# Softmax steps of the eighth b placed inside the last stage's h tiles, state rows stored from SyncE, output copies dealt out anew

## The chip, the cores and the metric

One core of a Trainium2 chip runs the whole program. The metric is the device time of one execution in microseconds, as the median of several executions; lower is better. The engines are named as in the profile: PE (TensorE), DVE (VectorE), ACT (ScalarE), POOL (GpSimd) and SP (SyncE, which issues nearly all transfers).

## What is computed

Three blocks follow one another. `x` is 8 x 8 x 512 x 64, `state` 8 x 8 x 32 x 64; after the first block there are 8 b's of 512 token rows and 32 state rows each, 512 wide.

```python
# attention between the tokens and the state, both ways
a  = softmax(x @ state.T / 8);   xread = a @ state
a2 = softmax(state @ x.T / 8);   sread = a2 @ x
# a wide layer with a clipped quadratic
h = x @ w_in                                   # 512 -> 2048
g = where(h >= 1, h, where(h <= -1, 0, (h + 1) ** 2 / 4))
x = g @ w_out                                  # 2048 -> 512
# soft mixture: 8 experts with 4 slots each
logits = x @ phi                               # 4608 x 32
d = softmax(logits, axis=0);  slot_input = d.T @ x
slot_out[e] = relu(slot_input[e] @ w1[e]) @ w2[e]
out = softmax(logits, axis=1) @ slot_out
```

All data are 32-bit floats. The softmax over axis 0 runs over all 4608 rows, so the experts can start only when the last row is in.

## The kernel before

The kernel works in stages b = 0 to 7, one for each b's 512 tokens, and a last stage b = 8 for the 256 state rows of all b's. In a stage, 16 h tiles (m = 0 to 15, `hstep`) of 128 hidden units each are multiplied on PE; ACT, DVE and POOL turn each into its part of g. In stage 8 an h tile is 12 matmuls of 128 x 256 (line 547, numbered k = 0 to 11): `w_in`'s columns are split in a high and a low part by `wsplit` one tile ahead, into two alternating buffers, on the engines that a table names. The h tiles have three PSUM banks in turn.

`estep(b, k)` multiplies four g tiles into the logits E (four groups to a b; the last group of b runs in stage b + 1). `smblock(b)` then does the running softmax over rows in steps, a generator that the stage's loop steps on:

1. eS is copied out of E (ACT).
2. LR, a group of eight matmuls that turn eS; then the maximum bm and nm (DVE), the exponential back into eS (ACT), and small copies.
3. dRp, four transposes of eS on PE, copied to dR (ACT).
4. `fall`: 64 matmuls of dR with `gp`, the buffer that holds this b's g, into the banks FV and FX; eight DVE instructions add them to `acc`.
5. for b = 7 alone, `merge`: Mp, P and Sp on PE fold the four partial accumulators; after it the places of `gp` and `acc` are given to loads of expert weights.

In stage 8 of the kernel before, the loop steps the block of b = 7 on once after each of the h tiles m = 1, 2, 3, 4, 5. Stages 2 to 7 have PE's order written out by hand. Stage 8 has not: there a planner orders every engine's instructions by priority (program order, with raised priority inside a group) and by the times of a model, so that a step can stand some matmuls behind its place in the text.

Expert weights (w1 and w2, 16 slices of 1 MB each) are loaded by SP into whatever place falls free (`give`, `prefetch`, line 820); most of the places come from this very stage: the `gp` units after `fall`, `acc` after P, the `win` buffers after the last splits that read them, the split buffers after the last h tile, the buffers of transposed g after the group P of `smstate`. SP works in order, so a load whose place is not free yet holds up the loads behind it.

At the end `combine` multiplies the slot outputs with the token weights into four PSUM banks at a time (two of one V tile and two others, or two X, one E, one H), copies the banks to `o` by DVE and ACT in turn (line 1138), and stores `o`: b's 0 to 5 in two column halves, b's 6 and 7 whole. The state rows (b = 8, two banks) are stored by eight POOL transfers of 64 KB each, between the stores of b = 6 and b = 7.

Of the kernel before, what the change touches and what calls it, by code (L numbers as in the profile page):

```python
# [13 lines left out]
PSUM = bass.MemoryType.PSUM  # L14


CFG = {'gg': 1, 'ns': 1, 'do': 0, 'no': 1, 'nl': 0, 'n0': (1, 12), 'nw': 512, 'nj': 'CABD', 'cw': (2, 2, 2, 4, 5, 6, 6, 7, 8, 8, 9, 11, 12, 13, 14, 15), 'pr': (0, 3, 4, 6), 'a0n': 4, 'w1p': (), 'r0': 3, 'sw': 1, 'whole': (6, 7), 'em': 8, 'lE': (0, 5, 8, 11), 'sV': (0, 4, 9, 12), 'sE': (7, 11, 15), 'sS': (1, 3, 5, 7), 'sN': 13, 'sM': (14, 14), 'gv7': 'EESEESSEEESSEEEE', 'cpos': (0, 0, 1, 1, 2, 2, 3, 7, 8, 9, 10, 10, 13, 14), 'at0': (4, 4, 7, 7, 9, 13, 14, 15, 15, 15), 'lP0': ((1, 1), (2, 1), (3, 1)), 'lP1': ((1, 0), (1, 1), (2, 0), (2, 1), (3, 0)), 'gv1': 'EEEEEEEEEESEEEES', 'f32': (0, 1, 2, 3), 'wsm': 14, 'xsP': 1, 'eng': ('PE',), 'wt8': (7, 8, 9, 10, 11, 12, 13, 14), 'wte': 'DA', 'wb': 12, 'gv6': (3, 5, 15), 'lP': ((0, 0), (0, 1), (1, 0), (2, 0), (3, 1)), 'attA': (3, 4, 7, 9, 9, 9, 11, 12), 'attB': (1, 11, 11, 12, 13), 'attN': (14, 15), 'dv': (3, 7, 8), 'fl': -0.484375, 'hp': 2000, 'att7': (3, 5, 6, 7, 8, 10), 'og': 1, 'n3': 1, 'n3m': 10, 'wS': ('AP', 'PP', 'AD', 'AP', 'DP', 'DP', 'PP', 'DD', 'AP', 'DP', 'AD', 'AP', 'DD', 'AD', 'DD', 'DP'), 'xsm': 12, 'k0': 0, 'rg': 6, 'spg': 0, 'att0': 6, 'att': 7, 'V0': (1, 3, 4), 'Vn': (0, 3, 9), 'Vx': 12, 'wn': 'H', 'wsev': 'adad', 'conv': (4, 8, 9, 11, 12, 13, 19, 21, 24, 26, 28, 32, 36, 40, 44, 48, 52, 56, 60), 'todo': [1, 1, 1, 2, 0, 0, 0, 3, 0, 0, 2, 2, 1, 1, 0, 0], 'E0': ((0, 8), (0, 14), (0, 14), (0, 15)), 'T0': ((0, 12), (0, 14), (0, 15), (1, 0)), 'sm0': 6, 'E': 1, 'sm': 1, 'tqB': (5, 9, 13), 'GP': 0, 'pe': (3,), 'psH': 3, 'gtpX': (0, 7), 'tq0': (13, 15), 'keep': (2, 3, 4, 5), 'x2': (1, 3), 'natm': 1, 'warm': 26, 'bounce7': (0, 3), 'split': 1, 'wt': 0, 'so': '111000000000ccc111111', 'smm': (0, 0, 1, 2, 8, 10, 12), 'tqv': (), 'tqvm': 0, 'first': 'x', 'apath': 2, 'f32c': 1, 'place': 1, 'attm': (3, 6, 7, 8, 9, 12), 'subPm': True, 'loDm': False, 'bounce': (0, 1, 2, 3), 'bq': ('s', 's'), 'xq': 's', 'nat': ((1, 11), (2, 2), (2, 3), (2, 11), (3, 2), (3, 4), (3, 9), (4, 2), (4, 3), (4, 9), (5, 2), (5, 3), (5, 9), (6, 2), (6, 4), (6, 9)), 'subP': (1,), 'mulD': (), 'loD': (), 'qlag': 0, 'gv0': 'ESSESEEESEEEEEEE', 'gv': 'EEEEEEESEEEESEEE', 'gvS': 'BEBBBEEESSSBEBBB'}


@with_exitstack  # L20
def kernel(
# [157 lines left out]
        stage_load(nxt(i))  # L179

    wps, wD = {}, {}

    def conv_wo(i):

        g, h = divmod(i - 8, 2)
        if h == 0:
            wD[g] = rot_g.tile([128, 4, 512], F32, tag="g", name="wD")
        words(i, wD[g][:, 2 * h:2 * h + 2, :].rearrange("p k f -> p (k f)"))
        stage_load(nxt(i))
        if h == 1:  # L190
            wps[g] = psX.tile([128, 512], F32, tag="X", name="wps")
            group([dict(out=wps[g][32 * k:32 * k + 32, :], lhsT=phi_t[:, k, :], rhs=wD[g][:, k], start=True, stop=True)
                   for k in range(4)], [made[0], made[1]])
            sb = rot_q.tile([128, 512], F32, tag="q", name="wsb")
            act(sb, wps[g])
            wpp = wps[g][:, 0:128].rearrange("p (x n) -> p x n", x=4)
            for x in range(4):
                mm(out=wpp[:, x, :], lhsT=sb[:, 128 * x:128 * x + 128], rhs=R4, start=True, stop=True)
            act(wp[:, 4 * g:4 * g + 4, :], wpp)

    def nat_load(u, at):
        if u < 8:
# [321 lines left out]
    def hstep(b, m):  # L524
# [105 lines left out]
    def smblock(b):  # L630
# [89 lines left out]
    def fall(b, al, dR):  # L720
# [226 lines left out]
    for b in range(B + 1):  # L947
# [14 lines left out]
        for m in range(NM):  # L962
# [156 lines left out]
    def combine(dh, groups):  # L1119
# [4 lines left out]
        for n, bs in groups:  # L1124
# [80 lines left out]
```

## Time and profile before

| | |
|---|---|
| median of 3 executions | 477.71 us (477.7 to 478.51) |
| the profiled execution | 476.62 us |
| its span in the trace | 474.8 us |
| PE busy | 92% of the span |
| DVE, ACT, POOL busy | 79%, 61%, 52% |
| transfers issued by SP (q1) | 93.00 MB |
| transfers issued by POOL (q0) | 0.52 MB |

The trace is that of the profiled execution; its times are counted from the start of the span. A busy share is an average over stages with different limits, so it is read stage by stage. Stage 8's h tiles start at about 363 us; the stores end at about 472 us.

### The profile page before, as it was taken

Reading aid. Unit: us, or ns where it says so; the run is one execution under the profiler, and the core shown is the slowest. Engines: PE = TensorE matmul, PEld = TensorE weight load, DVE = VectorE, ACT = ScalarE, POOL = GpSimd, SP = SyncE. Lnnn points to the kernel's source line nnn. Section 1 sums busy time; section 2 is a strip of 40 time slices with the busy share of each in tenths; the row PEclk is TensorE's granted clock in tenths of the full one; section 3 lists DMA queues with packets and bytes.
Section 4 is the critical chain, followed back from the end, with each engine's and each line's share of the span. In section 5 each row is a group of like instructions: output and inputs, shape, how many; then the busy total and the mean of one; then the engine's idle time right before and its main releaser. Section 6 shows DMA issues by size and latency. Waiting matters only on the chain.

```text
span 474.8 us, 10761 instructions
## 1 busy us (share of the span) xinstructions
PE 436.8 (92%) x4352; PEld 249.5 (53%) x4352; DVE 372.8 (79%) x664; ACT 288.6 (61%) x526; POOL 245.4 (52%) x222
## 2 busy tenths in 40 slices
PE   4699999999999999999999999999999998899860
PEld 2433345455565565565556555655656786436430
DVE  2999999896999998999899999977877665350350
ACT  1868987647784875887587588545745364210350
POOL 4243347865873973796397379645247542030030
PEclk9889899999999999999999999999999999999995
DMA  8999822010403613260361326106045399999998
GB/s 300 420 420 418 362 90 90 11 80 13 167 1 135 232 79 135 90 222 10 130 247 62 134 90 233 79 19 249 1 179 186 126 373 353 342 421 418 388 357 273
DMA packets 21634, 94.21 MB, mean 198 GB/s; under 512 B 1873, under 2 KB 8401, under 8 KB 13265
## 3 DMA queue, kind: packets, MB, share of 16 engines
q1 hardware_dynamic: 21328, 93.00, 51.9%
q8 instruction: 34, 0.56, 0.5%
q0 software_dynamic: 256, 0.52, 0.4%
q14 instruction: 16, 0.12, 0.1%
HBM read 80.41 MB, written 13.11 MB: 197 GB/s over the span
## 4 chain that ended last, share of the span: by engine, by line
PE 51%; DVE 29%; DMA 7%; issue 4%; POOL 3%; ACT 2%; ACTq 0%; SPq 0%; POOLq 0%; DVEq 0%
PE h L539 19%; DMA w<-in_w_dram 6%; DVE gp L618 6%; DVE g L593 5%; PE h L547 5%; PE E L116 4%; PE FV L122 4%; PE V L116 3%; PE FX L122 2%; PE h L530 2%; POOL c L569 2%; DVE mx L295 2%; PE FV L116 1%; DVE win L173 1%; DVE z L336 1%
## 5 line engine op out<-in xcount | busy, mean ns | idle before, releaser
L539 PE MATMUL h<-a,v 128*128 128x512 f32 x672 | 175.2, 404 | 2.0 <-DVE g L593 1.7
L569 POOL TENSOR_TENSOR c<-c 128x512 f32<-128x512 f32 x107 | 116.8, 1095 | 99.7 <-ACT c L128 97.9
L539 PEld LDWEIGHTS h<-a,v 128*128 128x128 f32 x672 | 120.3, 188 | 77.2 <-issue 19.7
L128 ACT ACTIVATE c<-h,half 128x512 f32<-128x512 f32 x128 | 88.2, 690 | 71.7 <-PE h L539 55.8
L593 DVE SCALAR_TENSOR_TENSOR g<-h,c 128x512 f32<-128x512 f32 x112 | 74.7, 668 | 19.7 <-POOL c L569 16.9
L618 DVE STREAM_TRANSPOSE gp<-g 128x512 f32<-128x512 f32 x112 | 78.2, 700 | 1.2
L486 POOL TENSOR_TENSOR v<-Vs,v 128x512 fp32r<-128x512 f32 x30 | 41.7, 1389 | 9.3 <-ACT Vs L128 9.3
L128 ACT ACTIVATE v<-V 128x512 fp32r<-128x512 f32 (+1 forms) x64 | 38.1, 602 | 6.8 <-PE V L122 3.8
L116 PE MATMUL V<-win,st_t 64*32 64x512 f32 x64 | 33.4, 601 | 4.0 <-ACT att L128 3.5
L122 PE MATMUL V<-win,st_t 64*32 64x512 f32 x448 | 35.7, 601 | 0.0
L530 PE MATMUL h<-spare,v 128*128 128x512 f32 x64 | 34.0, 669 | 1.8 <-DVE gp L593 0.8
L122 PE MATMUL FX<-gp,dR 32*32 32x512 f32 x512 | 35.6, 598 | 0.0
L122 PE MATMUL FV<-gp,dR 32*32 32x512 f32 x496 | 35.4, 597 | 0.0
L122 PE MATMUL E<-g,wp 128*32 128x512 f32 x168 | 29.5, 602 | 0.0
L116 PE MATMUL E<-g,wp 128*32 128x512 f32 x56 | 29.1, 602 | 0.0
L338 POOL TENSOR_TENSOR att<-att,z 128x512 f32<-128x512 f32 x16 | 17.2, 1077 | 18.1 <-DVE z L337 18.1
L547 PE MATMUL h<-XSh,v 128*128 128x256 f32 x128 | 25.2, 289 | 0.0
L1141 DVE COPY o<-oV 128x512 f32<-128x512 f32 x6 | 4.1, 692 | 26.6 <-PE oH L122 26.5
L128 ACT ACTIVATE spare<-wb 128x512 uint8<-128x512 uint8 x32 | 23.9, 784 | 0.0
L530 PEld LDWEIGHTS h<-spare,v 128*128 128x128 f32 x64 | 12.2, 207 | 20.8 <-issue 12.9
L547 PEld LDWEIGHTS h<-XSh,v 128*128 128x128 f32 x128 | 20.3, 189 | 2.8 <-issue 1.0
L1149 POOL DMA_DIRECT2D out_dram<-o x8 | 4.1, 518 | 31.8 <-DVE o L1141 31.8
(245 smaller groups left out, 829.9 us busy)
## 6 DMA issues: line engine op xcount, KB each, us to landing
w<-in_w_dram SPq DMA_DIRECT2D x22, 1024.0 KB, 10.1
xn<-in_xn_dram SPq DMA_DIRECT2D x8, 1024.0 KB, 4.8
wb<-in_won_dram SPq DMA_DIRECT2D x8, 1024.0 KB, 5.0
xs<-in_xs_dram SPq DMA_DIRECT2D x7, 1024.0 KB, 5.1
gp<-in_w_dram SPq DMA_DIRECT2D x6, 1024.0 KB, 6.8
out_dram<-o SPq DMA_DIRECT2D x12, 512.0 KB, 6.5
gp<-in_wout_dram SPq DMA_DIRECT2D x5, 1024.0 KB, 12.2
wb<-in_win_dram SPq DMA_DIRECT2D x4, 1024.0 KB, 13.6
```

The source lines that it names most:

```text
L116: first = mm(**calls[0])
L122: e = mm(**c)
L128: return nc.scalar.activation(out=out, in_=in_, func=func, **kw)
L295: nc.vector.tensor_reduce(out=mx, in_=S[G], op=ALU.max, axis=AX.X)
L338: (nc.vector if b in CFG["mulD"] else nc.gpsimd).tensor_tensor(out=t3, in0=t3, in1=z1.unsqueeze(2).to_broadcast([128, 16, 32]), op=ALU.mult)
L486: nc.gpsimd.tensor_tensor(out=lo[:, G, :], in0=Vs, in1=hi[:, G, :], op=ALU.subtract)
L530: mm(out=h, lhsT=Vt[0, c][0][:, G, 128 * mm_:128 * mm_ + 128], rhs=araw[0][G], start=(G == 0), stop=(G == 1))
L539: mm(out=h, lhsT=v[:, G, f], rhs=a[:, G, :], start=(k == 0), stop=(k == 5))
L547: mm(out=h, lhsT=w[:, j, :], rhs=x[:, j, :], start=(k == 0), stop=(k == 11))
L569: nc.gpsimd.tensor_tensor(out=c, in0=c, in1=c, op=ALU.mult)
L593: gI[b, m] = nc.vector.scalar_tensor_tensor(out=g, in0=h, scalar=1.0, in1=c, op0=ALU.max, op1=ALU.min)
L618: nc.vector.transpose(out=gd_of(b, m), in_=gT[b, m])
```

## The change

Three things change; two further ones (`fd`, `fa` and `fb`: delayed weight folding, extra warming matmuls) are added to the code but switched off by their values.

- `s8` and `s9`: in stage 8 the loop steps the block of b = 7 on only after tiles 1 and 5 (its steps 1 and 5). Steps 2, 3 and 4 are taken inside `hstep`: LR before matmul k = 7 of tile 2, dRp before k = 1 of tile 4, `fall` before k = 10 of tile 4. The matmul at that place is tied behind the last matmul of the step in PE's order.
- `st`: the state rows are stored by four SP transfers, one for each 32-partition strip (two b's each), in place of eight POOL transfers.
- `ev`: of four banks, 0 and 1 (the V tile, or the two X) are copied by DVE and 2 and 3 by ACT, where the two took turns before.

```diff
-CFG = {'gg': 1, 'ns': 1,
+CFG = {'ev': 1, 'st': 1, 'fa': 0, 'fb': 0, 's8': ((2,7),(4,1),(4,10)), 's9': (1, 5), 'fd': (), 'gg': 1, 'ns': 1,
...
             for j in range(4):
                 for w, x in ((wh, xh), (wh, xl), (wl, xh)):
-                    mm(out=h, lhsT=w[:, j, :], rhs=x[:, j, :], start=(k == 0), stop=(k == 11))
+                    e = None
+                    if (m, k) in CFG["s8"]:
+                        step(run["sm"])
+                        e = run["pe"]
+                    i = mm(out=h, lhsT=w[:, j, :], rhs=x[:, j, :], start=(k == 0), stop=(k == 11))
+                    if e is not None:
+                        tc.add_manual_dep(i.ins, e.ins.name, ORDER, reason="in turn")
                     k += 1
...
-        group([dict(out=LR[32 * t:32 * t + 32, :], ...
+        run["pe"] = group([dict(out=LR[32 * t:32 * t + 32, :], ...
...
-            nc.tensor.transpose(dRp[:, r, :], eS[:, 128 * r:128 * r + 128], ident)
+            run["pe"] = nc.tensor.transpose(dRp[:, r, :], eS[:, 128 * r:128 * r + 128], ident)
...
-        group([dict(out=F[k][32 * t:32 * t + 32, :], ...
+        run["pe"] = group([dict(out=F[k][32 * t:32 * t + 32, :], ...
...
-                        sm = smblock(b - 1)
+                        sm = run["sm"] = smblock(b - 1)
...
-            if sm is not None and (m >= CFG["sm0"] if b == 1 else m >= CFG["sm"] if last or CFG["smm"] is None else m in CFG["smm"]):
+            if sm is not None and (m >= CFG["sm0"] if b == 1 else (m in CFG["s9"] if CFG["s8"] else m >= CFG["sm"]) if last else m in CFG["smm"]):
                 step(sm)
...
-                if n_ev % 2:
+                if t > 1 if CFG["ev"] and T == 4 else n_ev % 2:
                     act(o[:, t], v)
                 else:
                     nc.vector.tensor_copy(out=o[:, t], in_=v)
...
+                elif CFG["st"]:
+                    ob = out.rearrange("(t q n) d -> n q t d", t=2, q=4)
+                    for q in range(4):
+                        dma(out=ob[512:544, q, :, dc], in_=o[32 * q:32 * q + 32, :, 0])
                 else:
                     for bb in range(B):
```

## Rows read from the trace of the kernel before

**Rows 1.** Chain that ended last, in order of time (start us, us, what).

```profile
412.77 11.56 DMA w<-in_w_dram
...
424.39 16.89 DMA w<-in_w_dram
```

**Rows 2.** Stretches: busy of each engine, granted clock, transfer engines' share, GB/s.

```profile
372.00:380.00 8.00, 8.00 (x161) 5.13 (x161) 4.63 (x10) 2.09 (x5) 3.38 (x4) 1.00 0.02 4
381.00:397.00 16.00, 15.95 (x142) 13.84 (x141) 11.14 (x26) 9.91 (x20) 7.20 (x7) 1.00 0.98 392
397.00:399.00 2.00, 2.00 (x20) 2.00 (x19) 0.85 (x2) 1.32 (x2) 0.18 (x1) 1.00 0.91 258
406.00:409.00 3.00, 2.73 (x44) 1.34 (x37) 0.87 (x2) 0.77 (x2) 0.52 (x1) 1.00 0.68 224
409.00:446.00 37.00, 35.27 (x457) 17.64 (x452) 11.44 (x18) 6.68 (x14) 5.14 (x3) 1.00 1.01 410
446.00:458.00 12.00, 9.96 (x102) 5.16 (x95) 5.67 (x10) 5.71 (x11) 2.97 (x6) 1.00 1.03 368
```

**Rows 3.** SP's issues in order of time; then its waits (total, times, longest us).

```profile
379.47 2.09 SPq L820 DMA_DIRECT2D gp<-in_w_dram  x4
...
397.21 0.33 SPq L820 DMA_DIRECT2D w<-in_w_dram  x1
...
406.73 0.33 SPq L820 DMA_DIRECT2D w<-in_w_dram  x1
...
454.67 9.37 SPq L1145 DMA_DIRECT2D out_dram<-o  x5
...
SPq L820 <- POOL v L521: 4.3, 1, 4.3
...
SPq L820 <- PE P L122: 6.0, 1, 6.0
```

**Rows 4.** The chain again, PE's part of it around the moved steps.

```profile
367.46 1.85 PE h L547 x14
...
369.67 2.80 PE h L547 x22
372.47 0.44 PE dRp L666 x4
372.90 1.52 PE h L547 x12
...
375.00 0.54 PE FV L116
...
379.39 3.03 PE h L547 x24
```

**Rows 5.** ACT and DVE in order of time, the instructions between the moved steps.

```profile
367.53 0.60 ACT L128 ACTIVATE eS<-E 128x512 f32<-128x512 f32 x1
...
370.99 0.69 ACT L128 ACTIVATE eS<-LR,nm 128x512 f32<-128x512 f32 x1 [0.35 <-PE h L547]
...
372.94 0.60 ACT L128 ACTIVATE dR<-dRp 128x512 f32<-128x512 f32 x1 [0.27 <-PE dRp L666]
...
375.23 0.94 DVE L521 TENSOR_TENSOR v<-win,v 128x512 fp32r<-128x512 f32 x1
...
379.40 1.66 DVE L742 SCALAR_TENSOR_TENSOR acc<-acc,al,FV 128x256 f32<-128x256 f32 x4 [2.89 <-PE FX L122]
380.97 1.65 DVE L742 SCALAR_TENSOR_TENSOR acc<-acc,al,FX 128x256 f32<-128x256 f32 x4
```

**Rows 6.** Queues (packets, MB, share of 16 engines), 457 to 465 us, then 464 to 472 us.

```profile
q1 hardware_dynamic: 816, 2.19, 74.6%
q0 software_dynamic: 256, 0.52, 25.4%
...
q1 hardware_dynamic: 2839, 2.82, 103.1%
```

**Rows 7.** ACT's first output copy of a four-bank set, in order of time.

```profile
453.56 0.60 ACT L128 ACTIVATE o<-oV 128x512 f32<-128x512 f32 x1 [1.95 <-DVE o L1141]
```

More of the change, by code (lines that the diff above doesn't have):

```diff
@@ L14 @@
 PSUM = bass.MemoryType.PSUM
-CFG = {'gg': 1, 'ns': 1, 'do': 0, 'no': 1, 'nl': 0, 'n0': (1, 12), 'nw': 512, 'nj': 'CABD', 'cw': (2, 2, 2, 4, 5, 6, 6, 7, 8, 8, 9, 11, 12, 13, 14, 15), 'pr': (0, 3, 4, 6), 'a0n': 4, 'w1p': (), 'r0': 3, 'sw': 1, 'whole': (6, 7), 'em': 8, 'lE': (0, 5, 8, 11), 'sV': (0, 4, 9, 12), 'sE': (7, 11, 15), 'sS': (1, 3, 5, 7), 'sN': 13, 'sM': (14, 14), 'gv7': 'EESEESSEEESSEEEE', 'cpos': (0, 0, 1, 1, 2, 2, 3, 7, 8, 9, 10, 10, 13, 14), 'at0': (4, 4, 7, 7, 9, 13, 14, 15, 15, 15), 'lP0': ((1, 1), (2, 1), (3, 1)), 'lP1': ((1, 0), (1, 1), (2, 0), (2, 1), (3, 0)), 'gv1': 'EEEEEEEEEESEEEES', 'f32': (0, 1, 2, 3), 'wsm': 14, 'xsP': 1, 'eng': ('PE',), 'wt8': (7, 8, 9, 10, 11, 12, 13, 14), 'wte': 'DA', 'wb': 12, 'gv6': (3, 5, 15), 'lP': ((0, 0), (0, 1), (1, 0), (2, 0), (3, 1)), 'attA': (3, 4, 7, 9, 9, 9, 11, 12), 'attB': (1, 11, 11, 12, 13), 'attN': (14, 15), 'dv': (3, 7, 8), 'fl': -0.484375, 'hp': 2000, 'att7': (3, 5, 6, 7, 8, 10), 'og': 1, 'n3': 1, 'n3m': 10, 'wS': ('AP', 'PP', 'AD', 'AP', 'DP', 'DP', 'PP', 'DD', 'AP', 'DP', 'AD', 'AP', 'DD', 'AD', 'DD', 'DP'), 'xsm': 12, 'k0': 0, 'rg': 6, 'spg': 0, 'att0': 6, 'att': 7, 'V0': (1, 3, 4), 'Vn': (0, 3, 9), 'Vx': 12, 'wn': 'H', 'wsev': 'adad', 'conv': (4, 8, 9, 11, 12, 13, 19, 21, 24, 26, 28, 32, 36, 40, 44, 48, 52, 56, 60), 'todo': [1, 1, 1, 2, 0, 0, 0, 3, 0, 0, 2, 2, 1, 1, 0, 0], 'E0': ((0, 8), (0, 14), (0, 14), (0, 15)), 'T0': ((0, 12), (0, 14), (0, 15), (1, 0)), 'sm0': 6, 'E': 1, 'sm': 1, 'tqB': (5, 9, 13), 'GP': 0, 'pe': (3,), 'psH': 3, 'gtpX': (0, 7), 'tq0': (13, 15), 'keep': (2, 3, 4, 5), 'x2': (1, 3), 'natm': 1, 'warm': 26, 'bounce7': (0, 3), 'split': 1, 'wt': 0, 'so': '111000000000ccc111111', 'smm': (0, 0, 1, 2, 8, 10, 12), 'tqv': (), 'tqvm': 0, 'first': 'x', 'apath': 2, 'f32c': 1, 'place': 1, 'attm': (3, 6, 7, 8, 9, 12), 'subPm': True, 'loDm': False, 'bounce': (0, 1, 2, 3), 'bq': ('s', 's'), 'xq': 's', 'nat': ((1, 11), (2, 2), (2, 3), (2, 11), (3, 2), (3, 4), (3, 9), (4, 2), (4, 3), (4, 9), (5, 2), (5, 3), (5, 9), (6, 2), (6, 4), (6, 9)), 'subP': (1,), 'mulD': (), 'loD': (), 'qlag': 0, 'gv0': 'ESSESEEESEEEEEEE', 'gv': 'EEEEEEESEEEESEEE', 'gvS': 'BEBBBEEESSSBEBBB'}
@@ new lines @@
+CFG = {'ev': 1, 'st': 1, 'fa': 0, 'fb': 0, 's8': ((2,7),(4,1),(4,10)), 's9': (1, 5), 'fd': (), 'gg': 1, 'ns': 1, 'do': 0, 'no': 1, 'nl': 0, 'n0': (1, 12), 'nw': 512, 'nj': 'CABD', 'cw': (2, 2, 2, 4, 5, 6, 6, 7, 8, 8, 9, 11, 12, 13, 14, 15), 'pr': (0, 3, 4, 6), 'a0n': 4, 'w1p': (), 'r0': 3, 'sw': 1, 'whole': (6, 7), 'em': 8, 'lE': (0, 5, 8, 11), 'sV': (0, 4, 9, 12), 'sE': (7, 11, 15), 'sS': (1, 3, 5, 7), 'sN': 13, 'sM': (14, 14), 'gv7': 'EESEESSEEESSEEEE', 'cpos': (0, 0, 1, 1, 2, 2, 3, 7, 8, 9, 10, 10, 13, 14), 'at0': (4, 4, 7, 7, 9, 13, 14, 15, 15, 15), 'lP0': ((1, 1), (2, 1), (3, 1)), 'lP1': ((1, 0), (1, 1), (2, 0), (2, 1), (3, 0)), 'gv1': 'EEEEEEEEEESEEEES', 'f32': (0, 1, 2, 3), 'wsm': 14, 'xsP': 1, 'eng': ('PE',), 'wt8': (7, 8, 9, 10, 11, 12, 13, 14), 'wte': 'DA', 'wb': 12, 'gv6': (3, 5, 15), 'lP': ((0, 0), (0, 1), (1, 0), (2, 0), (3, 1)), 'attA': (3, 4, 7, 9, 9, 9, 11, 12), 'attB': (1, 11, 11, 12, 13), 'attN': (14, 15), 'dv': (3, 7, 8), 'fl': -0.484375, 'hp': 2000, 'att7': (3, 5, 6, 7, 8, 10), 'og': 1, 'n3': 1, 'n3m': 10, 'wS': ('AP', 'PP', 'AD', 'AP', 'DP', 'DP', 'PP', 'DD', 'AP', 'DP', 'AD', 'AP', 'DD', 'AD', 'DD', 'DP'), 'xsm': 12, 'k0': 0, 'rg': 6, 'spg': 0, 'att0': 6, 'att': 7, 'V0': (1, 3, 4), 'Vn': (0, 3, 9), 'Vx': 12, 'wn': 'H', 'wsev': 'adad', 'conv': (4, 8, 9, 11, 12, 13, 19, 21, 24, 26, 28, 32, 36, 40, 44, 48, 52, 56, 60), 'todo': [1, 1, 1, 2, 0, 0, 0, 3, 0, 0, 2, 2, 1, 1, 0, 0], 'E0': ((0, 8), (0, 14), (0, 14), (0, 15)), 'T0': ((0, 12), (0, 14), (0, 15), (1, 0)), 'sm0': 6, 'E': 1, 'sm': 1, 'tqB': (5, 9, 13), 'GP': 0, 'pe': (3,), 'psH': 3, 'gtpX': (0, 7), 'tq0': (13, 15), 'keep': (2, 3, 4, 5), 'x2': (1, 3), 'natm': 1, 'warm': 26, 'bounce7': (0, 3), 'split': 1, 'wt': 0, 'so': '111000000000ccc111111', 'smm': (0, 0, 1, 2, 8, 10, 12), 'tqv': (), 'tqvm': 0, 'first': 'x', 'apath': 2, 'f32c': 1, 'place': 1, 'attm': (3, 6, 7, 8, 9, 12), 'subPm': True, 'loDm': False, 'bounce': (0, 1, 2, 3), 'bq': ('s', 's'), 'xq': 's', 'nat': ((1, 11), (2, 2), (2, 3), (2, 11), (3, 2), (3, 4), (3, 9), (4, 2), (4, 3), (4, 9), (5, 2), (5, 3), (5, 9), (6, 2), (6, 4), (6, 9)), 'subP': (1,), 'mulD': (), 'loD': (), 'qlag': 0, 'gv0': 'ESSESEEESEEEEEEE', 'gv': 'EEEEEEESEEEESEEE', 'gvS': 'BEBBBEEESSSBEBBB'}
@@ L181 @@
     wps, wD = {}, {}
+    pend = []
     def conv_wo(i):
@@ L196, in conv_wo, with over @@
             wpp = wps[g][:, 0:128].rearrange("p (x n) -> p x n", x=4)
-            for x in range(4):
-                mm(out=wpp[:, x, :], lhsT=sb[:, 128 * x:128 * x + 128], rhs=R4, start=True, stop=True)
-            act(wp[:, 4 * g:4 * g + 4, :], wpp)
+            def over():
+                for x in range(4):
+                    mm(out=wpp[:, x, :], lhsT=sb[:, 128 * x:128 * x + 128], rhs=R4, start=True, stop=True)
+                act(wp[:, 4 * g:4 * g + 4, :], wpp)
+            if g in CFG["fd"]:
+                pend.append(over)
+            else:
+                over()
     def nat_load(u, at):
@@ L263, with warm @@
     araw = {}
-    def warm(n):
+    def warm(n, after=None):
         w = psE.tile([128, 128], F32, tag="E", name="warm")
-        for _ in range(n):
-            mm(out=w, lhsT=xs_s[:, 1920:2048], rhs=xs_s[:, 1920:2048], start=True, stop=True)
+        with tc.high_priority(CFG["hp"] if after is not None else 0):
+            for _ in range(n):
+                x = ident if after is not None else xs_s[:, 1920:2048]
+                i = mm(out=w, lhsT=x, rhs=x, start=True, stop=True)
+                if after is not None:
+                    tc.add_manual_dep(i.ins, after.ins.name, ORDER, reason="in turn")
+                    after = i
     def attention(b):
@@ L324, in turn @@
                 for st in range(4):
-                    nc.tensor.transpose(p[:, st, :], e2[G][:, 128 * st:128 * st + 128], ident)
+                    i = nc.tensor.transpose(p[:, st, :], e2[G][:, 128 * st:128 * st + 128], ident)
+                if b == 0 and G == 0 and CFG["fa"]:
+                    warm(CFG["fa"], i)
                 t = e2[G].rearrange("p (a x) -> p a x", a=4)
@@ L468, in vchunk @@
         P2 = [slice(64 * G, 64 * G + 64) for G in range(2)]
-        group([dict(out=V[G][32 * j:32 * j + 32, :], lhsT=st_t[P2[G], b, j, :], rhs=win_t[c][P2[G], j, :],
-                    start=True, stop=True) for j in range(4) for G in range(2)])
+        i = group([dict(out=V[G][32 * j:32 * j + 32, :], lhsT=st_t[P2[G], b, j, :], rhs=win_t[c][P2[G], j, :],
+                        start=True, stop=True) for j in range(4) for G in range(2)])
+        if (b, c) == (0, 1) and CFG["fb"]:
+            warm(CFG["fb"], i)
         if b == 0 and c in CFG["f32"]:
@@ L639, in smblock @@
         LR = psX.tile([128, 128], F32, tag="X", name="LR")
-        group([dict(out=LR[32 * t:32 * t + 32, :], lhsT=R4, rhs=eS[:, 128 * t:128 * t + 128], start=True, stop=True) for t in range(T)])
+        run["pe"] = group([dict(out=LR[32 * t:32 * t + 32, :], lhsT=R4, rhs=eS[:, 128 * t:128 * t + 128], start=True, stop=True) for t in range(T)])
         bm = small.tile([128, 1], F32, tag="bm", name="bm")
@@ L731, in fall @@
             halves = [(slice(0, 8), slice(8, 16)), (slice(8, 16), slice(0, 8))]
-        group([dict(out=F[k][32 * t:32 * t + 32, :], lhsT=dR[32 * k:32 * k + 32, r, 32 * t:32 * t + 32],
+        run["pe"] = group([dict(out=F[k][32 * t:32 * t + 32, :], lhsT=dR[32 * k:32 * k + 32, r, 32 * t:32 * t + 32],
                     rhs=g[32 * k:32 * k + 32, t, r], start=(r == 0), stop=(r == 3))
@@ L973 @@
             hstep(b, m)
+            while pend:
+                pend.pop()()
             nat(b, m)
```

## Prediction

> **What bounds the kernel now.** I read the end of the span first. The chain of what ended last consists, from 412.77 us on, of two waits for loads of expert weights, 11.56 and 16.89 us [rows 1]. The stretches say why: from 409 us on the transfer engines are never free, with a share of 1.01 to 446 us and 1.03 to 458 us [rows 2], and by queue 74.6 + 25.4 = 100% in 457:465 and 103.1% in 464:472 [rows 6] (a packet is booked where it starts, so a share can pass 1). So from 409 us to the end, some 63 us, time is bytes divided by rate: it shortens only if there are fewer or cheaper packets, or if this stretch can begin earlier.
>
> When can it begin? Before it the same table shows holes: a share of 0.02 in 372:380, 0.91 at only 258 GB/s in 397:399, and 0.68 in 406:409 [rows 2]. A hole means that SP has nothing that it may issue. The issues tell what it waits for: at 379.47 the end of `fall`, after which four gp loads go out in 2.09 us; at 397.21 the last split that reads a `win` buffer (POOL v, a wait of 4.3 us); at 406.73 the group P of the last stage (PE P, 6.0 us) [rows 3]. So loads come in batches, each opened by a gate. The fall gate is the change's target. The two behind it hang on PE's h tiles, and the PE is without a pause there: 8.00 of 8.00 us in 372:380 and 15.95 of 16.00 in 381:397 [rows 2]. The reading that decides the case is that each gate finds the transfer engines dry. Whatever a batch gains by starting early, the next gate takes back.
>
> **The moved softmax steps.** What moves is order, not work: no matmul goes or comes. I count h matmuls ahead of each step from the chain [rows 4]. Two tiles (24) stand ahead of the E group that ends at 367.46; then 14 before LR, 22 to dRp, 12 to the E of the last stage. LR so has 38 ahead, dRp 60, `fall` 72 and one E group. In the new text LR has 24 + 7 = 31, dRp 48 + 1 = 49, `fall` 48 + 10 = 58 and no E of stage 8. An h matmul costs 2.80 / 22 = 0.127 us, the E group 375.00 - (372.90 + 1.52) = 0.58 us [rows 4]. LR starts 7 x 0.127 = 0.89 us earlier, dRp 11 x 0.127 = 1.40 us, `fall` 14 x 0.127 + 0.58 = 2.36 us.
>
> Are the inputs there by then? The copy eS ends at 367.53 + 0.60 = 368.13 [rows 5]; LR would start at 367.46 + 1.85 - 0.89 = 368.42: 0.29 us to spare. LR ended at 369.67 [rows 4], the exponential at 370.99 + 0.69 = 371.68 [rows 5], so that stretch takes at most 2.01 us; with LR's end now at 368.78 it is done by 370.79, and dRp would start at 372.47 - 1.40 = 371.07: 0.28 us to spare. The copy dR ended 373.54 - 372.91 = 0.63 us after dRp [rows 4, 5]; dRp now ends at 371.51, dR at 372.14, and `fall` would start at 375.00 - 2.36 = 372.64: 0.50 us. All three covers are h matmuls; if one is gone, what is tied behind the step stands with it. I take no wait there.
>
> What follows `fall` is less comfortable. Call its end T = 379.39 - 2.36 = 377.03. At T DVE turns to the eight additions to `acc`, 1.66 + 1.65 = 3.3 us [rows 5]. Before, tiles 4 and 5 had been copied out during `fall`, tile 7's split was made there on DVE too (its subtraction at 375.23 took 0.94 us [rows 5]), and PE found three free banks and ready weights. Now tile 4 has two matmuls left, so its copy, and the split for tile 7 (which may start when tile 5 is done), queue behind the additions on DVE. PE meanwhile has 2 + 12 + 12 h matmuls, 26 x 0.127 = 3.3 us, the E group, 0.58, and eight transposes of quarter 0 if they go ahead: T + 3.9 without them. DVE comes to the split at T + 3.3 and needs about 0.4 + 0.4 + 0.9 us for a copy, a cast and the subtraction: T + 5.0. That is a wait of up to 1.0 us, and near nothing if the transposes (some 0.8 us, which must run anyway) and the first two matmuls of tile 7, which don't read the subtraction, lie in it. I take 0.2 us, the end where they fill it, since all of that filling is ready by then. Below nothing I exclude more than 0.1 us: PE has no pause to give back. A pause of PE shifts the gates at 397.21 and 406.7 one for one, and with them the end.
>
> The four gp loads would be issued from 377.1 instead of 379.47, and the hole of 372:380 shrinks by 2.36 us. What is late next is the split of 397.21: the batch that opened with gp was through at about 397.8, as the fall in rate in 397:399 shows [rows 2]; now it is through at about 395.4, and the engines stand idle until the gate. Worth to the end: 0. It costs nothing either, since these loads are read only after 412.77 [rows 1].
>
> **The state rows.** In 457:465 q0's 256 packets, 0.52 MB, took 25.4% of 8 us, 2.03 us of all 16 engines, a rate of 258 GB/s; SP's stores in 464:472 moved 2.82 MB in 103.1% of 8 us, 8.25 us, a rate of 342 GB/s [rows 6]. At that rate the state rows take 1.53 us: a saving of 0.50 us of a stretch that is full. Bounds: 0, if they are as slow on the other queue, and 2.03 - 0.52 / 0.410 = 0.76 us, if they reach the 410 GB/s of the loads in 409:446 [rows 2]. A loss I exclude down to 0, because half the packets' extra time would have to come from SP's queue, whose smallest stores already do better. I take 0.50, the nearest row (the same SP queue, stores, the same stretch). Four issues enter SP's queue between the stores of b = 6 and b = 7. There five issues took 9.37 us, because the queue was full [rows 3]: SP waits for the transfer engines there, not they for SP. Eight issues leave POOL, and nothing stands behind them.
>
> The Trainium skill ("DMA: Bandwidth & Descriptors", section "Issuing engines are not separate DMA queues") speaks against a gain: transfers from whichever engine run on the same 16 transfer engines, and only issue time is saved. The trace bears out the shared engines (the two shares add up to 100% [rows 6]) but not the equal price, 258 against 342 GB/s. By the rule alone this term would be 0.
>
> **The output copies.** ACT's first copy of a set, at 453.56, ended a wait of 1.95 us for DVE's first copy of that set [rows 7]: both read the V tile. With V to DVE and the others to ACT nothing waits, and a set should be ready earlier by about what ACT now lags, less than one 0.60 us copy [rows 7]. The share is 1.03 in 446:458 [rows 2], so the engines have stores enough and the work that hides it is those. I take 0; if a set's store were awaited it would be some 0.5 us, once.
>
> **The sum** against the profiled execution (span 474.8, time 476.62): +0.2 - 0.5 + 0 = -0.3, 476.3 us. The median of the runs lies 1.1 us above that execution, so for a median I add the same difference to 477.71: 477.4 us. With the bounds (PE -0.1 to +1.0, state rows -0.76 to 0, copies -0.5 to 0) it runs from 476.35 to 478.7.
>
> **Rivals.**
> - *The early start is kept.* If the later gates were not what opens the last stretch, the 2.36 us would come off the end whole, with the state rows' 0.5: 474.9 us. For it: the hole in 372:380 is the largest of all [rows 2]. Against it: the holes at the two later gates. Chance 0.15.
> - *TensorE stands at the ties, slower than before.* PE works in order, so the h matmul tied behind `fall` and all behind it wait when a step's input is late. The covers are 0.28 to 0.50 us; one queued instruction of 0.6 to 0.9 us on DVE or ACT [rows 5] ahead of bm or dR uses one up and leaves about 0.4. Two such ties and the 1.0 us behind the additions make 1.8, less 0.5 for the state rows: 479.0 us. It decides as soon as PE loses more than 1.5 us between 363 and 400 us. For it: DVE's 3.3 us and the thin covers. Chance 0.17.
> - *The queues cost the same.* The 0.52 MB take their 2.03 us on either queue, because rows of one strip are slow by themselves: +0.2, 477.9 us. This is the skill's rule above as a mechanism. For it: q1's packets in 457:465 ran at 2.19 MB in 5.97 us, 367 GB/s, about as fast as otherwise, so it is the transfers' shape that may be slow. Chance 0.15.
> - *The change doesn't move `fall`.* The planner may fill the ties with matmuls of the next tile, since three banks are in turn, and `fall` ends where it did: -0.5 alone, 477.2 us. Chance 0.06.
>
> **How the numbers follow.** The forecast, 477.4, has 0.47. A measurement of this kernel can tell about 0.2%, 0.96 us, from no change: faster means under 476.75, slower over 478.67. Faster: the first rival's 0.15 and 0.12 of the forecast's lower part (dearer state rows, copies that count), 0.27. Slower: 0.14 of the second rival and 0.03 from upper ends of the others, 0.17. Within: 0.56. The range 475.8 to 479.0 leaves out the first rival and the upper part of the second, together about 0.2.
>
> **What would show it.** `fall` starting near 372.6 and gp loads issued near 377.1 show the move; a share well under 1 around 395:397 with the issue still at about 397.2 shows the gate. That issue or the one at 406.73 over 0.5 us later, or a pause of PE behind tile 6, shows the second rival. In the last 15 us q0 should be gone, with a rate above 340 GB/s throughout, and ACT's copies should no longer end a wait for DVE. The prediction is wrong if the issue near 406.7 comes over 1 us earlier, or if the share behind 409 us falls below 1.

## The result, and the profile after

The changed kernel takes 479.9 us (median of 20 runs, 476.9 to 483.2) against 477.4 us of the kernel before (20 runs beside it): a ratio of 1.0056, 95% interval 1.0039 to 1.0072. By the ratio it is slower by 2.7 us (1.9 to 3.4), by the two medians by 2.5, outside the range that was given. The profiled execution of it took 480.2 us with a span of 478.4 us.

The stretches after answer to [rows 2] (busy of PE, PEld, DVE, ACT, POOL, granted clock, transfer engines' share, GB/s):

```profile
372.00:380.00 8.00, 7.06 (x149) 4.42 (x148) 3.37 (x8) 0.68 (x2) 2.06 (x3) 1.00 0.15 20
381.00:397.00 16.00, 15.77 (x134) 14.01 (x133) 10.93 (x26) 9.82 (x19) 6.43 (x8) 1.00 1.00 404
397.00:399.00 2.00, 2.00 (x22) 1.45 (x21) 1.22 (x4) 0.63 (x2) 1.57 (x2) 1.00 0.14 57
406.60:410.40 3.80, 3.74 (x34) 1.56 (x34) 0.82 (x4) 0.01 (x1) 0.00 (x0) 0.55 0.60 253
410.00:446.00 36.00, 33.77 (x434) 16.19 (x430) 9.44 (x15) 5.49 (x12) 5.67 (x4) 1.00 0.97 389
446.00:458.00 12.00, 10.15 (x111) 5.27 (x110) 4.16 (x7) 4.76 (x10) 0.00 (x0) 1.00 0.92 337
450.00:452.00 2.00, 2.00 (x30) 1.13 (x28) 1.48 (x4) 0.72 (x2) 0.00 (x0) 1.00 0.47 176
```

PE was without a pause in 372:380 before [rows 2]; now it is busy 7.06 of 8.00 us. The hole at 397:399 is deeper (0.14 in place of 0.91), and a new one stands where before there was none: 0.47 in 450:452, in the middle of the stretch that was never to be free.

SP's issues after answer to [rows 3] (start us, us, line, what):

```profile
378.76 2.30 SPq L843 DMA_DIRECT2D gp<-in_w_dram  x4
...
399.13 3.43 SPq L843 DMA_DIRECT2D w<-in_w_dram  x4
...
410.31 1.28 SPq L843 DMA_DIRECT2D w<-in_w_dram  x3
...
450.17 9.14 SPq L1170 DMA_DIRECT2D out_dram<-o  x7
459.56 4.23 SPq L1174 DMA_DIRECT2D out_dram<-o  x4
```

The gp loads go out 0.71 us earlier than before (379.47), not 2.36; the gate at 397.21 comes at 399.13 (+1.92), that of group P at 410.31 in place of 406.73 (+3.58) [rows 3]. The two later gates moved by more than the first gained, in the wrong direction.

**Where the 1.92 us arise.** The chain that ended last, after (start us, us, what):

```profile
368.91 0.09 PE LR L116
...
370.48 1.13 DVE D L771
...
372.27 1.13 DVE sn L683
373.40 0.34 DVE s_gc L620
373.74 0.04 issue
373.79 0.50 PE h L568 x2
374.29 0.55 PE FV L116
...
380.26 1.65 DVE acc L765 x4
...
382.68 0.69 DVE v L538
383.37 0.34 DVE s_gc L620
383.72 0.04 issue
383.76 1.69 PE h L568 x12
```

Where the chain before had only PE [rows 4], DVE stands in it twice. First ahead of `fall`: two one- and four-column instructions of 1.13 us each, then the copy that frees tile 2's PSUM bank, and for that bank two h matmuls wait that the planner had put ahead of `fall`: they are the first two of tile 5, which fill up the tie. (LR, too, came after 9 matmuls of tile 2, not after 7: the planner let two of tile 2 go ahead.) Second behind `fall`: the first matmul of tile 7 waits at 383.76 for the copy that frees tile 4's bank (`s_gc`, ended 383.71). DVE made that copy behind the additions to `acc` and behind the subtraction for tile 7's split.

The timeline says why the two small instructions are long (start us, us, engine, line, operation, idle before in brackets); the first two rows are POOL's, the last two PE's:

```profile
370.29 1.29 POOL L538 TENSOR_TENSOR v<-win,v 128x512 fp32r<-128x512 f32 x1 [1.39 <-DVE v L537]
372.11 1.27 POOL L538 TENSOR_TENSOR v<-win,v 128x512 fp32r<-128x512 f32 x1 [0.53 <-DVE v L537]
...
370.40 1.21 DVE L771 TENSOR_SCALAR D<-cst_t,nm 128x4 f32<-128x4 f32 x1
...
372.19 1.20 DVE L683 SCALAR_TENSOR_TENSOR sn<-sn,al,bs 128x1 f32<-128x1 f32 x1
...
373.79 0.39 PE L568 MATMUL h<-XSh,v 128*128 128x256 f32 x1 [0.94 <-DVE s_gc L620]
...
383.76 0.39 PE L568 MATMUL h<-XSh,v 128*128 128x256 f32 x1 [0.23 <-DVE s_gc L620]
```

D starts 0.11 us after POOL's subtraction and ends with it (371.61 and 371.58); sn starts 0.08 us after the next one and ends with it (373.39 and 373.38). An instruction of some 0.2 us lasts as long as POOL's. The trace of before had the same thing, in rows that the prediction did not read (DVE's, then POOL's):

```profile
370.32 0.55 DVE L651 SCALAR_TENSOR_TENSOR nm<-bm,nm 128x1 f32<-128x1 f32 x1
370.90 0.23 DVE L748 TENSOR_SCALAR D<-cst_t,nm 128x4 f32<-128x4 f32 x1
...
372.04 0.90 DVE L660 SCALAR_TENSOR_TENSOR sn<-sn,al,bs 128x1 f32<-128x1 f32 x1
...
369.57 1.28 POOL L521 TENSOR_TENSOR v<-win,v 128x512 fp32r<-128x512 f32 x1 [0.62 <-DVE v L520]
371.63 1.29 POOL L521 TENSOR_TENSOR v<-win,v 128x512 fp32r<-128x512 f32 x1 [0.79 <-DVE v L520]
```

There nm and sn were held, D just missed it (370.90 against an end at 370.85), and no matmul stood behind them. The Trainium skill ("SBUF — State Buffer", section "SBUF: two separate sides") says that DVE and GpSimd share one pair of ports, and that a DVE instruction which needs it (one in a mode that takes both ports, or one with two inputs in SBUF beside a GpSimd instruction that reads SBUF) and a GpSimd instruction exclude each other: whoever starts first holds the pair for its whole instruction while the other stands still. The trace agrees: 1.21 us in place of 0.23. It does so all through the trace of before: each of the nine nm and sn of b = 1 to 7 that start under a POOL `tensor_tensor` ends within 0.03 us of its end, after 0.25 to 1.03 us; the five others take 0.17 to 0.18.

**What the end lost.** PE around the first output group (`oV`), after:

```profile
444.50 1.07 PE L1122 MATMUL SO<-w,hTD 128*32 128x256 f32 x16 [0.95 <-DMA w<-in_w_dram]
445.50 0.70 PE L1131 MATMUL SR<-tail,cst_t 128*128 128x256 f32 x2
447.07 0.64 PE L1122 MATMUL SO<-w,hTD 128*32 128x256 f32 x8 [0.87 <-DMA w<-in_w_dram]
447.64 0.48 PE L116 MATMUL oV<-tail,LT 32*128 32x256 f32 x1
```

and before, where SR stood ahead of the same 16 and no further weights came ahead of the group:

```profile
439.90 0.70 PE L1106 MATMUL SR<-tail,cst_t 128*128 128x256 f32 x2
441.33 1.07 PE L1097 MATMUL SO<-w,hTD 128*32 128x256 f32 x16 [0.73 <-DMA w<-in_w_dram]
442.33 0.48 PE L116 MATMUL oV<-tail,LT 32*128 32x256 f32 x1
```

The planner put one more weight slice ahead of the first output group; this order came with the moved steps (s8_only below has it, ev_st has not). That group waits for a load that lands at 447.03, the first store goes out at 450.17 (before 445.34), and until the stores start there is little to move: the hole of 450:452. At a share of 0.47 over 2 us the hole itself is some 1.1 us.

### The profile page after: what moved, and what is told of

Read it like the earlier page. It is cut to its first block, busy times and chain, and to the rows that moved or that the text cites. A ratio compares the mean times of both kernels' runs of the same rounds, so it can differ in the third digit from the quotient of the medians.

```text
span 478.4 us, 10753 instructions
## 1 busy us (share of the span) xinstructions
PE 438.8 (92%) x4352; PEld 249.6 (52%) x4352; DVE 372.5 (78%) x664; ACT 288.6 (60%) x526; POOL 241.5 (50%) x214
## 4 chain that ended last, share of the span: by engine, by line
PE 47%; DVE 25%; DMA 14%; ACT 4%; issue 4%; POOL 3%; SPq 1%; DVEq 0%; POOLq 0%; ACTq 0%
PE h L556 19%; DMA w<-in_w_dram 6%; DVE gp L641 6%; DMA wb<-in_win_dram 6%; DVE g L616 5%; PE E L116 4%; PE h L568 4%; PE FV L122 4%; PE V L116 3%; PE FX L122 2%; PE h L547 2%; DMA out_dram<-o 2%; POOL c L592 2%; PE FV L116 1%; DVE z L351 1%
## 5 line engine op out<-in xcount | busy, mean ns | idle before, releaser
L1166 DVE COPY o<-oV 128x512 f32<-128x512 f32 x12 | 7.7, 686 | 27.9 <-PE oH L122 27.8
L391 POOL TENSOR_TENSOR a<-att,a 128x512 fp32r<-128x512 f32 x14 | 19.6, 1424 | 1.1 <-ACT a L128 1.1
```

The source lines that it names most:

```text
L391: (nc.vector if b in CFG["loD"] or b > 1 and CFG["loDm"] else nc.gpsimd).tensor_tensor(out=lo[:, G, :], in0=raw[G], in1=hi[:, G, :], op=AL ...
```

## The experiments

All times in the tables are read from the trace of each kernel and counted from its first h matmul of the last stage, so that what happened earlier drops out (one profile each). `fall`, h tiles, P: their end on PE; first store: its issue; last: end of the last packet on the two queues that carry the stores (q1 and q0).

| kernel | median us | ratio to before (95%) | fall | h tiles | P | first store | last |
|---|---|---|---|---|---|---|---|
| before | 477.4 | 1 | 16.03 | 36.12 | 43.34 | 81.98 | 109.90 |
| after | 479.9 | 1.0056 (1.0039, 1.0072) | 15.37 | 38.07 | 46.96 | 86.86 | 113.76 |
| s8_only | 480.14 | 1.0055 (1.0033, 1.0076) | 15.36 | 38.07 | 45.29 | 85.49 | 112.79 |
| st_only | 476.31 | 0.9974 (0.9960, 0.9989) | 16.02 | 36.12 | 43.34 | 81.43 | 108.87 |
| ev_only | 477.43 | 0.9996 (0.9981, 1.0012) | 16.02 | 36.12 | 43.34 | 82.39 | 109.62 |
| ev_st | 475.93 | 0.9975 (0.9956, 0.9994) | 16.00 | 36.08 | 43.30 | 82.35 | 109.40 |
| tiny_on_act | 478.56 | 1.0017 (1.0001, 1.0034) | 14.17 | 36.87 | 45.74 | 85.92 | 112.80 |
| tie_h5 | 476.63 | 0.9992 (0.9976, 1.0007) | 13.92 | 36.62 | 45.12 | 82.63 | 110.81 |
| tail_do | 477.19 | 1.0005 (0.9985, 1.0026) | 15.36 | 38.05 | 45.27 | 81.88 | 110.15 |
| fixed_all | 476.40 | 0.9982 (0.9964, 1.0000) | 13.93 | 36.37 | 43.59 | 80.20 | 108.42 |
| tail_do_again | 477.62 | 1.0013 (0.9992, 1.0035) | 15.38 | 38.09 | 45.31 | 81.93 | 110.10 |
| tail_do_fill | 477.87 | 1.0004 (0.9985, 1.0022) | 15.37 | 38.07 | 45.29 | 81.91 | 110.16 |
| ev_st_do | 475.65 | 0.9969 (0.9946, 0.9991) | 16.03 | 36.12 | 43.34 | 79.96 | 108.22 |
| st_pool4 | 478.15 | 1.0018 (1.0002, 1.0033) | 16.02 | 36.12 | 43.34 | 81.39 | 110.01 |

**The parts one by one.** The changed kernel with only one or two of its parts.

```diff
 s8_only: 'ev': 0, 'st': 0, 's8': ((2,7),(4,1),(4,10))
 st_only: 'ev': 0, 'st': 1, 's8': ()
 ev_only: 'ev': 1, 'st': 0, 's8': ()
 ev_st:   'ev': 1, 'st': 1, 's8': ()
```

> The moved softmax steps alone; state rows and output copies as before. Theory A (the moved steps make PE stand: one wait of about 1.1 us ahead of fall for a PSUM bank whose copy is late, about 0.5 us at tile 7, and the clock at its lower level during P): the whole loss is here, about 479.9 us, with the last h tile ending near 401.4 instead of 399.5. Theory B (the loss comes at the end, from the state rows in SP's queue and the other order of the copies): about 477.4 us.

> The state rows by four SP transfers alone. Theory A: the state rows' packets take 1.82 us of all transfer engines (changed kernel) instead of 2.03, so 477.2 us, about 0.2 us less than before. Theory B: 1 us or more slower, 478.5 us, with a hole in the transfer engines' share between the last load and the first store.

> The output copies dealt out anew, alone. Theory A: within 0.3 us of before, 477.4 us; ACT's first copy of a set no longer ends a wait for DVE and the first store goes out about 0.5 us earlier. Theory B: slower by up to 1 us.

> State rows and output copies changed together, softmax steps as before. Theory A: 477.0 to 477.4 us, no slower than before. Theory B: about 479.9 us, all of the loss.

The whole loss is in the moved steps (1.0055 alone); the copies are worth nothing that can be measured; the stores gain 0.26%, 1.2 us, and keep it beside the copies. st_only and ev_st came out below both of their expectations, and ev_only's first store came 0.41 us later, not 0.5 earlier. Beside the moved steps the gain of the stores does not show: the changed kernel (1.0056) is no faster than s8_only (1.0055), where 1.0030 would follow from adding up. The three intervals together allow for the difference.

**The small instructions off DVE.** D, and sn of the last b, go to ACT; all else, the planner's order on PE and at the end included, stays.

```diff
-        nc.vector.tensor_scalar(out=D, in0=blk, scalar1=nmo, scalar2=None, op0=ALU.mult)
+        act(D, blk, scale=nmo)
...
+            if b == B - 1:
+                act(run["s"], so, ACTF.Identity, scale=al, bias=bs)
+            else:
                 nc.vector.scalar_tensor_tensor(out=run["s"], in0=so, scalar=al, in1=bs, op0=ALU.mult, op1=ALU.add)
```

> The changed kernel with two one-column or four-column instructions of b = 7 (D of merge and the sum sn) on ACT instead of DVE; PE's order is the same. Theory C (these two are held on DVE until POOL's running subtraction ends, 1.2 us each in the changed kernel's trace, and so make the copy of tile 2 late, for whose bank PE then waits 1.1 us ahead of fall): that wait shrinks to 0.3 us or less, the last h tile ends about 1 us earlier than in the changed kernel, 478.9 us. Rival D (the wait is that of the three banks and the additions, whatever POOL does): as the changed kernel, 479.9 us, and fall starts where it did.

Two rows of ACT, and PE's last h matmul ahead of `fall` with the start of `fall`, in this kernel:

```profile
371.11 0.29 ACT L128 ACTIVATE D<-cst_t,nm 128x4 f32<-128x4 f32 x1
...
371.70 0.38 ACT L128 ACTIVATE sn<-sn,bs,al 128x1 f32<-128x1 f32 x1
...
373.00 0.28 PE L568 MATMUL h<-XSl,v 128*128 128x256 f32 x1
373.21 0.61 PE L116 MATMUL FV<-gp,dR 32*32 32x512 f32 x1
```

D's 0.29 us lie inside a POOL subtraction (370.49 to 371.78); sn's 0.38 us fall almost wholly between that one and the next, which starts at 372.23. PE's pause ahead of `fall` is gone, and `fall` and the h tiles end 1.20 us earlier (14.17 for 15.37, 36.87 for 38.07). Of the time 1.0056 - 1.0017 = 0.39% goes. So D and sn in DVE's queue were the cause of that pause; that POOL's subtraction made them long is read from their starts and ends above.

**The tie closed, the end's order set, and all of it.** tie_h5 ties the first matmul of tile 5 behind `fall`, so that it can't fill the tie; tail_do ties the weight slices of the second half behind the first output group; fixed_all does both, has the small instructions on ACT, and gives tile 7's split to ACT and POOL in place of DVE.

```diff
 tie_h5, fixed_all:
                     if (m, k) in CFG["s8"]:
                         step(run["sm"])
                         e = run["pe"]
+                    if (m, k) == (5, 0):
+                        e = run["pe"]
 tail_do, fixed_all:
-'do': 0
+'do': 1
 fixed_all: the table of splits 'wS', entry of tile 7
-'DD'
+'AP'
```

> The changed kernel with the first matmul of tile 5 tied behind fall, so that PE reaches fall without waiting for tile 2's bank. This also gives the end of the kernel the order of before (SR ahead of the slice that stands before the first output group). Theory C: no wait ahead of fall (1.1 us), fall 1 us earlier; with the order at the end (about 0.9 us) 477.9 us. Rival D: the wait only moves behind fall, PE's h tiles end where they did in the changed kernel, 479.0 us.

> The changed kernel with the slot-output matmuls of the second half tied behind the first group of output matmuls, so that no load stands ahead of the first store. Theory E (about 0.9 us of the loss is the hole before the stores, where the first output group waits for one weight slice more than before): the hole goes, 479.0 us or a little less. Rival F (the stores come after all loads anyway): 479.9 us.

> The changed kernel with D and sn on ACT, tile 5 tied behind fall, the split of tile 7 on ACT and POOL instead of DVE, and the output order as in the run with the first group ahead. PE should lose nothing beside before, and fall should end over 2 us earlier. Theory G (the next gate takes an early start of the gp loads back): as with state rows and copies alone, 475.5 to 476 us. Rival H (the early start is kept once PE doesn't wait): 473.5 to 474 us.

tie_h5 ends the h tiles 1.45 us earlier than the changed kernel, but it is no test of that alone: with it the planner went back to the order of before at the end too (first store 82.63), so it repairs both; its 476.63 us are below what either theory expected. tail_do repairs the end alone: PE's loss of 1.9 us stays (38.05), the first store comes at 81.88, and the hole is filled:

```profile
450.00:452.00 2.00, 1.30 (x14) 0.41 (x6) 0.00 (x0) 0.55 (x2) 0.00 (x0) 1.00 1.09 385
```

It takes 0.5% less time than the changed kernel, some 2.4 us, where 0.9 was expected. Its order goes beyond that of before: 176 of the SO matmuls stand ahead of the first output group, against 208 before and 216 in the changed kernel. fixed_all is the answer to what the move itself is worth. Its `fall` ends 2.10 us earlier than before and PE has lost only 0.25 us at the end of the h tiles. Its stretches and SP's issues:

```profile
395.00:397.00 2.00, 2.00 (x22) 1.45 (x21) 1.25 (x4) 0.43 (x2) 1.57 (x2) 1.00 0.55 234
397.00:399.00 2.00, 2.00 (x19) 2.00 (x19) 0.85 (x2) 1.34 (x3) 0.30 (x1) 1.00 0.44 78
```

```profile
377.21 2.36 SPq L848 DMA_DIRECT2D gp<-in_w_dram  x4
...
397.33 0.33 SPq L848 DMA_DIRECT2D w<-in_w_dram  x1
...
406.82 6.06 SPq L848 DMA_DIRECT2D w<-in_w_dram  x5
```

gp is issued at 377.21, near the predicted 377.1; the transfer engines have run dry in 395:397 (0.55), and the gates stand at 397.33 and 406.82 as before. The gain of the first gate is taken back by the second. The 476.40 us of fixed_all lie a little above the 475.5 to 476 of theory G and far from the 473.5 to 474 of rival H.

**Is it the clock, the number of slices, or the queue?** In the profile of the changed kernel PE's granted clock was 0.55 in 406.6:410.4, that is mostly its lower level of 1.2 GHz, after waits of 1.08, 1.31 and 0.31 us between 401.8 and 406.7, and group P took 3.61 us where it took 1.93 before. tail_do_fill puts idle matmuls into those pauses. ev_st_do has the end's tie without the moved steps. st_pool4 stores the state rows with the change's four transfers, but from POOL.

```diff
 tail_do_fill (to tail_do): three after the last h tile, five after LRs, each tied behind the one before
+                mm(out=w, lhsT=ident, rhs=ident, start=True, stop=True)
 ev_st_do (to ev_st)
-'do': 0
+'do': 1
 st_pool4 (to st_only)
-                        dma(out=ob[512:544, q, :, dc], in_=o[32 * q:32 * q + 32, :, 0])
+                        nc.gpsimd.dma_start(out=ob[512:544, q, :, dc], in_=o[32 * q:32 * q + 32, :, 0])
```

> The changed kernel with the first output group tied ahead of the remaining weight slices, again, as the near neighbour of the next kernel. Expected by all theories: as on the other chip, 477.2 us with single runs from 475 to 480.5; group P takes 1.9 us or, where the granted clock falls to 0.5 in it, about 3.5.

> The kernel above with eight idle matmuls of 128 x 128 in TensorE's pauses of the last softmax (three after the last h tile, five after LRs), whose result nobody reads; nothing else differs in any engine's order. Clock theory: the long runs of the changed kernel are those in which group P runs at the lower clock level (3.5 in place of 1.9 us), because TensorE stands still for some microseconds ahead of it; then P takes 1.9 us here, no run is above 479, and the median is 0.3 to 1.5 us under that of the kernel above. Rival: the pauses have no part in it, the spread is that of the transfers of the last 60 us; then median and highest run are the same as above within 0.4 us. Second rival: the eight matmuls push the work behind them back; P ends up to 0.5 us later and the median is up to 0.5 us higher.

> Stores and copies as changed, softmax steps as before, and the first output group tied ahead of the remaining weight slices. Theory: in the order of the kernel before, the first output group already stands where its inputs are there as early as that, the loss at the end belongs to the planner's new order in the changed kernel alone; then 475.9 us, ratio 0.997 to 0.998, first store within 0.5 us of the 82.4 us after the first h matmul of stage 8. Rival: any weight slice less ahead of the first group is worth its own loading time at the end; then about 1 us less, 474.9 us, ratio 0.9955, first store 1 us earlier.

> The kernel before with the state rows stored by four transfers of one strip each, as in the change, but issued by POOL; copies and softmax steps as before. It parts the two things that the store change did at once (another queue, half as many transfers). Theory Q: what the change of stores gained, 1.2 us, came from the queue, since two queues in the last 15 us slow each other's packets; then this kernel stays at 477.5 us, ratio 0.999 to 1.001. Theory N: it came from the number of transfers; then 476.3 us, ratio 0.9975.

The filled pauses change nothing that can be told: medians 477.62 and 477.87, P at the full clock in both profiles. The highest run is lower (479.1 against 480.6), from 12 runs each, which is too few to speak for the clock. What share the lower clock has in the changed kernel's long runs stays open; s8_only was as slow (480.14) with P at full clock in its profile (there the clock was 0.50 in 432.4:435.8). The mean granted clock of each run points to a share, but does not show it: of the changed kernel's 20 runs the eight at 0.975 or less took 480.2 to 483.2 us (median 482.5), the other twelve 476.9 to 480.4 (median 479.1). The kernel before shows no such split (477.0 and 477.5 in its 35 runs beside the last four kernels). Where in the long runs the clock fell no trace shows.

ev_st_do issues its first store 2.4 us earlier than ev_st and its time is the same within the intervals (0.9969 and 0.9975). Neither theory expected an earlier store that gains nothing. It is the fastest kernel here, by a hair, and the neighbour against which tail_do is read: they differ in the moved steps alone, and PE's 1.93 us (38.05 for 36.12) return in P (+1.93), first store (+1.92), last transfer (+1.93) and median (+1.5, and +2.0 in the second run). So what PE loses in the h tiles is paid once, in full.

st_pool4 has the same four transfers as st_only and none of the gain: 1.0018 against 0.9974. The queues of the two in 455:463, st_pool4 first:

```profile
q1 hardware_dynamic: 473, 2.19, 71.4%
q0 software_dynamic: 184, 0.51, 27.3%
...
issues: line engine op xcount, KB each, median us to landing
...
out_dram<-o POOLq DMA_DIRECT2D x4, 128.0 KB, 6.6
```

```profile
q1 hardware_dynamic: 881, 2.89, 98.3%
...
out_dram<-o SPq DMA_DIRECT2D x4, 128.0 KB, 4.2
```

0.51 MB from POOL took 27.3% of 8 us, 2.18 us, or 234 GB/s, and land in 6.6 us; from SP they land in 4.2 us, and q1, which then carries them, moves 2.89 MB there where the two queues together moved 2.70 (2.19 + 0.51). So the number of transfers is not the cause; the queue is.

## Why the prediction was wrong, step by step

**The term that failed: PE +0.2 us, bounds -0.1 to +1.0.** It measured +1.95 us (36.12 to 38.07), and the outcome of the second rival, TensorE standing at the ties, took place, though by another cause: not a step's input was late but the bank of a matmul that filled the tie. Of it 1.20 us are the wait ahead of `fall` (what tiny_on_act gives back), some 0.4 the wait at tile 7, the rest small ones. The step that failed is "if one is gone, what is tied behind the step stands with it. I take no wait there". I had checked only whether the inputs of LR, dRp and `fall` are there in time, and they were. I had not asked what the planner would put ahead of `fall`, though the last rival named it: 11 matmuls, two of them of tile 5, whose bank was free only after DVE. And I gave DVE's small instructions no price at all, though nm and sn stood in the trace with 0.55 and 0.90 us.

**The wait behind the additions** was right in its place and its sign, at the start of tile 7; I took 0.2 us of a bound of 1.0, and PE's matmuls start 0.51 us apart there (383.25 and 383.76) where 0.12 is normal, a wait of some 0.4. PE waited there for tile 4's bank, not for the split: the subtraction stood ahead of the bank's copy on DVE.

**What the prediction did not see: the end.** No term of the sum was for the order of the weight slices and output groups at 440 to 450 us. The moved steps don't touch it in the text; the planner sets it, and it came out otherwise in the changed kernel, s8_only and tiny_on_act, not in tie_h5. It was put at nothing without a reason, and with it fails the reading that the transfer engines are never free behind 409 us: their share is 0.47 in 450:452. By tail_do it is worth 2.1 to 2.4 us (1.0056 to 1.0013 and 1.0005). Other neighbours give less: the last transfer of tail_do comes 3.6 us before the changed kernel's, of which 1.7 are the lower clock in P, so 1.9; and from s8_only less the 0.25% of stores and copies (1.0030) to tail_do it is 0.8 to 1.2 us. So the cause is shown, but its size only as about 1 to 2.4 us, and part of the upper figure may be the clock's.

**The sum, set right.** Stores and copies in tail_do's order of the end -0.31% (ev_st_do), -1.5 us; PE +1.9; the end's order +2.1 to 2.4: together +2.5 to +2.8 us, where +0.56%, 2.7 us, was measured. Only PE's term is read from a trace; the other two are differences of the same runs, so that the sum tests PE's term alone.

**The moved `fall`**: start 372.64, end 377.03 predicted, 374.22 and 378.7 measured, since the pause of 1.2 us lies ahead of it. With the pause gone it starts 2.1 us earlier. That this is worth 0, because the gate of the last splits takes it back, was right: fixed_all and ev_st_do, with 2.1 us between their `fall`s and the same tie at the end, have their last transfer at 108.42 and 108.22. The first rival, the early start kept, falls with that.

**The state rows**: -0.50 us predicted, 0 to -0.76; measured 0.26%, 1.2 us (0.5 to 1.9 by the interval). The sign was right, and the queue is the cause (st_pool4); that the size was too small is not shown, since 0.50 lies at the edge of the interval. The working was wrong in its rate: the 256 packets take 1.82 us in the trace of after for 2.03 before [rows 6], 288 GB/s and not 342, which is only 0.2. By the last transfers the gain is 1.03 us in st_only. Of these, 0.48 lie between the first store and the last transfer (27.44 for 27.92) and 0.55 ahead of the first store, where the change of stores does nothing; I take that part for the scatter of single profiles. That q1's packets run slower beside q0 is not the rest: 2.19 MB in 71.4% of 8 us are 383 GB/s; 2.89 MB alone in 98.3% are 367, and some 390 without the state rows among them (0.52 MB in 1.82 us). What makes up the gain beyond 0.2 us stays open. The five issues in 9.37 us were misread as a full queue alone: between 454.7 and 464 us SP also waited 3.3 us for DVE's copies and 2.0 for ACT's. The Trainium skill ("DMA: Bandwidth & Descriptors", section "Issuing engines are not separate DMA queues") would give 0 here, as the third rival had it. st_only and st_pool4 differ in the issuing engine alone and by 0.44%: the measurement decides against it for these stores.

**The copies**: 0 predicted, 0.9996 measured (0.9981 to 1.0012). As predicted, ACT's copies no longer wait for DVE (the first in the trace of after, at 448.86, ends a wait for PE).

**What would show it** named the issue near 397 or 406.73 over 0.5 us later as the mark of the second rival: it came 1.92 and 3.58 us later, of the latter 1.7 us by the lower clock in P. The prediction's own sign of being wrong, a share below 1 behind 409 us, came too: 0.97 in 410:446 and 0.92 in 446:458.

## What to carry to other kernels

A step tied into an in-order engine's stream brings along whatever the planner places ahead of the tie: ask of each of those instructions when its bank comes free, not only of the moved step when its inputs are there. Read the durations of an engine's smallest instructions in the trace of before: one of 0.9 us where its like takes 0.2 can mark a resource that someone else holds, and a move can put it on the critical path. Where a planner orders part of the program, a change of one stage can reorder another 70 us later; compare the orders of all engines, and tie the order that matters.

## What the runs showed of the hardware

- A DVE instruction of one to four columns of the forms of nm, sn (`scalar_tensor_tensor` on SBUF) and D (`tensor_scalar`) that starts under a POOL `tensor_tensor` lasts until that ends: 1.20 and 1.21 us in place of some 0.2. The one-input forms of b = 0 (nm from bm, sn from bs) did not: 0.11 and 0.15 us under POOL's work at 91.2 and 92.4 us. On ACT D took 0.29 us inside a POOL subtraction.
- State rows stored by POOL cost more of the transfer engines' time than by SP: 234 to 258 GB/s against 288 (0.52 MB in 1.82 us), and the kernel 0.26 to 0.44% in time.
- PE's granted clock fell to its lower level in group P in the profiles of the changed kernel, tiny_on_act and tie_h5 (P took 3.6, 3.6 and 3.2 us), and not in those of s8_only, tail_do and fixed_all (1.9 us), with the same work and the same pauses ahead of it (1.08, 1.31 and 0.31 us).
